# Computing integer angles and their quarter-turn shift on GpSimd instead of ScalarE and VectorE

## The chip, the cores and the metric

The kernel runs on one core of a Trainium2 chip. The metric is device time in microseconds (us). The engines are called PE (TensorE), ACT (ScalarE), DVE (VectorE), POOL (GpSimd) and SP (SyncE, which issues the DMAs).

## The reference, cut to what matters

A state-space convolution (S4) of 2048 steps and 512 channels with 128 states is mixed by a gate with a routed feed-forward update of two tokens. Only this part concerns the change:

```python
dt = jnp.exp(log_dt)[:, None]
A = A_re + 1j * A_im
logdA = dt * A                                          # (D=512, N=128)
l = arange(L) cast to bfloat16
P = jnp.exp(logdA[:, :, None] * l[None, None, :])       # complex powers
K = jnp.einsum("dn,dnl,dn->dl", C, P, dt * B).real      # the convolution's kernel
y = irfft(rfft(u padded) * rfft(K padded))              # long convolution
...
return g * a + (1 - g) * b
```

The kernel builds `P` as a product of two tables: lag t = t1 + t2, one table of exp(dt·A·t1), one of exp(dt·A·t2). Each entry is a magnitude (an exponential on ACT) times a sine or a cosine of an angle.

## The kernel before

The kernel describes its work as a list of operations with costs, and a list scheduler in the kernel's own source places them on the engines before anything is compiled; the engines then run fixed orders and wait on semaphores. A changed cost or engine therefore also changes the order. Channels come in two halves, `h` = 0 and 1.

The angles are 16-bit integers, 65536 to a turn, so that wrapping is free. There are 16 groups of four angles, eight groups for each half. `B16` holds the base angle as float32:

```python
def trig(h, angs, ts, neg):
    k = na[0] % 2                                   # two angle buffers, used in turn
    na[0] += 1
    a, ah, s = ARG[k], ARH[k], SNC[k]
    for i, t in enumerate(angs):                    # 4 scalings of 256, f32 -> int32
        SCL(a(0, 128, i * HC, (1, HC)), B16(0, 128, h * HC, (1, HC)), float(t), [B16], [(a, i)])
    ks = [(a, i) for i in range(4)]
    ...
    AC(so(0), lo, ACTF.Sin, ks, [(s, "s")], scale=SC16, tset=ts)      # sine of the low 16 bits
    w = a(0, 128, 0, (1, n))
    TS(w, w, 16384.0, ALU.add, ks, ks)              # a quarter turn: 1 add of 1024 int32
    AC(so(2), lo, ACTF.Sin, ks, [(s, "c")], scale=SC16, tset=ts)      # cosine
```

`SCL` may go to ACT or DVE, as the scheduler finds; `TS` is on DVE. The sines and cosines feed long rows of DVE multiplies (`TT`, two inputs in SBUF, bf16), of 2048, 1024, 512 or 1280 elements a partition:

```python
def TT(o, a, b, op, rd, wr, **k):
    return P.op(DVE, lambda h: h.tensor_tensor(out=o, in0=a, in1=b, op=op), rd, wr, cost=tt_cost(o, a, b), **k)
```

Memory is reused tightly. One reuse matters below: the second half's tables `TQ[1]` lie where the product table `KA[0]` of the first half lies.

```python
TQ = [... for i, o in enumerate((oE, oG))]
KA = [B("ka0", oG, 64 * 84 * 2), B("ka1", oE, 64 * 84 * 2)]
...
tab1(0, (1, 1)); forward(); tab2(0, (1, 1)); tab1(1, (1, 1)); xupd(); kgen(0); tab2(1, (1, 1)); ...; kgen(1); ...
```

So `tab2(1)` on DVE can't write before the results of `kgen(0)`, matmuls of the first half's tables whose products go to `KA[0]`, have been read out of there. PE runs the forward transform (`forward`), which needs no tables.

Of the kernel before, what the change touches and what calls it, by code (L numbers as in the profile page):

```python
# [14 lines left out]
ALU = mybir.AluOpType  # L15
AX = mybir.AxisListType

PE, ACT, DVE, POOL, SP = "pe", "act", "dve", "pool", "sp"
# [237 lines left out]
BLK, NBLK, HF, HC = 1024, 2, 2, 256  # L256
# [70 lines left out]
def bass_gated_mix__ssm_conv_s4__moe_arch_mod__prompt_kernel(nc, A_u, A_A_re, A_A_im, A_B_re, A_B_im, A_C_re, A_C_im, A_log_dt, A_Dskip,  # L327
# [24 lines left out]
    with ExitStack() as es:  # L352
# [6 lines left out]
        P = Prog()  # L359
# [18 lines left out]
        def nel(ap):  # L378
            r = 1
            for s, c in ap.ap[1:]:  # L380
                r *= c
            return r
# [5 lines left out]
        def TS(o, a, s1, op0, rd, wr, s2=None, op1=None, rate=0.5e-3, **k):  # L388
            c = 0.17 + nel(o) * rate
            if op1 is None:  # L390
                return P.op(DVE, lambda h: h.tensor_scalar(out=o, in0=a, scalar1=s1, scalar2=None, op0=op0), rd, wr, cost=c, **k)  # L391
            return P.op(DVE, lambda h: h.tensor_scalar(out=o, in0=a, scalar1=s1, scalar2=s2, op0=op0, op1=op1), rd, wr, cost=c, **k)
# [4 lines left out]
        def AC(o, a, func, rd, wr, scale=1.0, bias=0.0, **k):  # L397
            return P.op(ACT, lambda h: h.activation(out=o, in_=a, func=func, scale=scale, bias=bias), rd, wr,  # L398
                        cost=0.185 + nel(o) * 0.833e-3 + (0.09 if not isinstance(scale, float) else 0), **k)
# [4 lines left out]
        def SCL(o, a, c, rd, wr, **k):  # L404
            n = nel(o)
            return P.op((ACT, DVE), (lambda h: h.activation(out=o, in_=a, func=ACTF.Copy, scale=c), lambda h: h.tensor_scalar(out=o, in0=a, scalar1=c, scalar2=None, op0=ALU.mult)), rd, wr,  # L406
                        cost=(0.19 + n * 0.833e-3, 0.165 + n * (0.48e-3 if a.dtype == F32 else 0.245e-3)), **k)
        def DMA(pairs, rd, wr, nbytes, eng=SP, **k):
            return P.op(eng, lambda h: [h.dma_start(o, i) for o, i in pairs], rd, wr, cost=0.5 * len(pairs), n=len(pairs), nbytes=nbytes, dma=True, **k)

# [67 lines left out]
        def DQ(pairs, rd, wr, nbytes, **k):  # L478
            dp[0] -= 1e3
            return DMA(pairs, rd, wr, nbytes, prio=dp[0], **k)  # L480
# [60 lines left out]
        def trig(h, angs, ts, neg):  # L541
            k = na[0] % 2
            na[0] += 1
            a, ah, s = ARG[k], ARH[k], SNC[k]
            for i, t in enumerate(angs):
                SCL(a(0, 128, i * HC, (1, HC)), B16(0, 128, h * HC, (1, HC)), float(t), [B16], [(a, i)])
            ks = [(a, i) for i in range(4)]
            lo = bass.AP(ah.tensor, ah.offset, [[ah.ap[0][0], 128], [2 * HC, 4], [8, 64], [2, 4]])
            n = 4 * HC
            def so(k):  # L550
                return s(0, 128, k * n, (4, 4), (16, 64), (1, 4))
            AC(so(0), lo, ACTF.Sin, ks, [(s, "s")], scale=SC16, tset=ts)
            w = a(0, 128, 0, (1, n))
            TS(w, w, 16384.0, ALU.add, ks, ks)
            AC(so(2), lo, ACTF.Sin, ks, [(s, "c")], scale=SC16, tset=ts)
            if neg:
                SCL(s(0, 128, n, (1, n)), s(0, 128, 0, (1, n)), -1.0, [(s, "s")], [(s, "n")])
            return s
        def tab1(h, ts):
            for g in range(4):  # L560
                s = trig(h, ANG1[4 * g:4 * g + 4], ts[g // 2], True)
                n = 4 * HC
                ti, tr = TP[h]
                ek = [(tr, ("e", 4 * g + i)) for i in range(4)] + [(tr, ("e", 16 + 4 * g + i)) for i in range(4)]
                v = lambda b: b(0, 128, 16 * g, (64, 2), (128, 64), (1, 16))
                TT(v(ti), v(tr), s(0, 128, 0, (n, 2), (16, 64), (1, 16)), ALU.mult, ek + [(s, "s"), (s, "n")], [(ti, g)])
                TT(v(tr), v(tr), s(0, 128, 2 * n, (0, 2), (16, 64), (1, 16)), ALU.mult, [(s, "c")], ek)
# [17 lines left out]
        def tab2(h, ts):  # L585
# [3 lines left out]
            for g in range(4):  # L589
                s = trig(h, ANG2[4 * g:4 * g + 4], ts[g // 2], False)  # L590
                if g < 2:
                    im, re = [b_(0, 128, 16 * g, (4 * NJ, 64), (1, 16)) for b_ in (qi, qr)]
                    src = eb(0, 128, 16 * g, (32, 64), (1, 16))
                    ek = [(eb, ("e", 4 * g + i)) for i in range(4)]
                    ki, kr = (qi, ("s", g)), (qr, ("s", g))
                else:
                    im, re = [b_(0, 128, 16 * (g - 2), (32, 64), (1, 16)) for b_ in (bi, br)]
                    src = re
                    ek = [(br, ("e", 4 * (g - 2) + i)) for i in range(4)]
                    ki, kr = (bi, ("i", g)), (br, ("r", g))  # L600
                TT(im, src, s(0, 128, 0, (16, 64), (1, 16)), MUL, ek + [(s, "s")], [ki])
                TT(re, src, s(0, 128, 2 * n, (16, 64), (1, 16)), MUL, ek + [(s, "c")], [kr] + (ek if g > 1 else []))
                if g < 2:
                    v = lambda part: tq(part)(0, 128, 16 * g, (4 * NJ, 64), (4, 4), (1, 4))
                    w = lambda part: WW(0, 128, (1 - part) * D + h * HC, (4, 64), (0, 4), (1, 4))
                    cmul(h, v, v, w, n, [ki, kr], [WW], lambda p: [(ki, kr)[p]])
# [11 lines left out]
        def routing():  # L618
# [75 lines left out]
            for i, (W, k) in enumerate(((wg, [WG]), (wu, WU))):  # L694
# [7 lines left out]
                P.op(PE, ffn1, [*k, XS], [bb.buf], cost=56 * 0.026)  # L702
                CP(hb(i), bb(0, 128, 0, (1, 28)), [bb.buf], [(HB, i)])
            DMA([(WD(0, 128, 0, (D, 14), (1, D)), dr(B_w_down, 0, (D, 128), (128 * D, 14), (1, D)))], [], [WD], 1835008)
            AC(hb(2), hb(0), ACTF.Silu, [(HB, 0)], [(HB, 2)], tset=1)
            TT(hb(3), hb(2), hb(1), MUL, [(HB, 2), (HB, 1)], [(HB, 3)])
# [11 lines left out]
        def forward():  # L718
            np_ = [0]
            for blk in range(NBLK):  # L720
                for ft in range(4):
                    k = blk * 4 + ft
                    ng = NG[k % 2]
                    if k > 1:
                        DMA([(ng(0, 128, 0, (128, 8), (1, 128)), ngsrc(ft))], [], [ng], 262144, prio=2e5)
                    for pm in range(2):
                        pb = fwp[np_[0] % 2]
                        np_[0] += 1
                        for part in range(2):
                            def fw(h, blk=blk, ft=ft, pm=pm, pb=pb, ng=ng, part=part):  # L730
                                last = None
                                o = pb(0, 128, part * 512, (1, 512))
                                for par in range(2):
                                    for st in range(4):
                                        w = ng(0, 128, (st * 2 + part) * 128, (1, 128)) if par and pm else F(0, 128, ((par * 4 + st) * 2 + part) * 512 + ft * 128, (1, 128))
                                        last = h.matmul(o, w, U(0, 128, (blk * 8 + st * 2 + par) * D, (1, D)), start=(par + st == 0), stop=(par * 4 + st == 7 and blk == 0))  # L736
                                if blk:
                                    last = h.matmul(o, CB(0, 128, 640 if part == 0 else 512, (1, 128)),  # L738
                                                    X(0, 128, (1 - part) * 2048 + (pm * 4 + ft) * 256, (8192, 2), (1, 256)), start=False, stop=True)
                                return last  # L740
                            rd = [F, CB, ng] + [(U, blk * 8 + t) for t in range(8)]
                            if blk:
                                rd += [xk(hh, 0, 1 - part, pm, ft) for hh in range(2)]
                            P.op(PE, fw, rd, [(pb.buf, part)], cost=(8 + blk) * 0.217)
                        EV(X(0, 128, blk * 4096 + (pm * 4 + ft) * 256, (2048, 2), (8192, 2), (1, 256)), pb(0, 128, 0, (512, 2), (256, 2), (1, 256)),
                           [pb.buf], [xk(hh, blk, part, pm, ft) for hh in range(2) for part in range(2)])
# [204 lines left out]
```

## Time and profile before

206.42 us, median of three runs (206.23 to 206.93); the profiled span is 203.5 us.

| What | Value |
|---|---|
| DVE busy / PE busy / ACT busy / POOL busy | 171.3 / 163.9 / 141.1 / 3.4 us |
| angle scalings on ACT, on DVE | 44 x 407 ns, 20 x 284 ns |
| quarter-turn adds on DVE | 16 x 680 ns |
| DVE multiplies of 1024, of 2048 | 681 ns, 1216 ns |
| second half's `kgen` matmuls start | 137.56 us |

The window view, busy microseconds of each engine in chosen stretches of the kernel before (after the stretch: its length, then PE, PE weight loads, DVE, ACT, POOL with instruction counts, then the granted clock, the DMA share and GB/s):

```profile
40.00:60.00 20.00, 19.76 (x191) 10.13 (x192) 19.93 (x38) 18.90 (x31) 0.00 (x0) 1.00 0.42 119
60.00:80.00 20.00, 19.89 (x92) 9.10 (x93) 20.00 (x38) 19.62 (x32) 0.00 (x0) 1.00 0.13 30
80.00:104.60 24.60, 24.44 (x255) 14.43 (x257) 20.74 (x31) 22.48 (x38) 0.00 (x0) 1.00 0.25 89
104.60:116.70 12.10, 8.40 (x26) 2.56 (x25) 12.06 (x21) 12.03 (x21) 0.00 (x0) 0.72 0.53 228
116.70:137.60 20.90, 12.57 (x111) 10.31 (x110) 20.90 (x35) 8.27 (x9) 0.00 (x0) 0.91 0.00 1
```

From 40 to 104.6 us three engines are full. From 104.6 to 137.6 us DVE is full and PE is not.

The groups, kernel before (count, then busy us and mean ns of one, then idle time before and who ended it): first the page's group of all multiplies, then the groups by shape:

```profile
L387 DVE TENSOR_TENSOR AR<-AR 128x1024 bf16<-128x1024 bf16 (+7 forms) x184 | 135.7, 797 | 12.5 <-DMA AR<-in_A_A_re_dram 6.8
L387 DVE TENSOR_TENSOR AR<-AR 128x2048 bf16<-128x2048 bf16 x48 | 57.3, 1216 | 0.1
L387 DVE TENSOR_TENSOR AR<-AR 128x1024 bf16<-128x1024 bf16 x90 | 57.0, 681 | 5.2 <-ACT AR L398 4.4 <-PE ps L775 0.6
L406 ACT ACTIVATE AR<-AR 128x256 int32<-128x256 f32 x44 | 15.3, 407 | 0.1
L391 DVE TENSOR_SCALAR AR<-AR 128x1024 int32<-128x1024 int32 x16 | 10.9, 680 | 0.0
L406 DVE TENSOR_SCALAR AR<-AR 128x256 int32<-128x256 f32 x20 | 4.8, 284 | 1.9 <-ACT AR L398 1.8
```

The second and third are most of the table and product multiplies; the last three are what the change moves. The PE timeline, the line where the second half's `kgen`, matmuls of its tables, begins (start, length, and in brackets the idle time before it):

```profile
137.56 7.81 PE L756 MATMUL ps<-AR 128*128 128x84 bf16 x128 [7.60 <-DVE AR L387]
```

PE waited 7.60 us for a DVE multiply here. From this line to the end are 66 us.

### The profile page before, as it was taken

How to read it: one execution, taken by the hardware profiler on the slowest of the kernel's cores; microseconds unless marked ns; L12 is line 12 of the kernel's file. 1: busy time of each engine (PE TensorE's matmuls, PEld its weight loads, DVE VectorE, ACT ScalarE, POOL GpSimd, SP SyncE). 2: the span in 40 equal slices, each digit the busy share in tenths (PEclk: the TensorE clock that was granted, in tenths of full speed). 3: DMA queues.
4: the chain of work that ended last, by engine and by line, in shares of the span. 5: the costliest groups of instructions: out<-in, count | busy, mean ns of one | idle time of the engine just before them, and what ended most of it. 6: DMA issues, size and time to landing. Idle time of an engine off the chain costs nothing.

```text
span 203.5 us, 3609 instructions
## 1 busy us (share of the span) xinstructions
PE 163.9 (81%) x1479; PEld 108.6 (53%) x1490; DVE 171.3 (84%) x281; ACT 141.1 (69%) x232; POOL 3.4 (2%) x7
## 2 busy tenths in 40 slices
PE   0084799999999999999984999509889999809992
PEld 0073544774344444466550387408668888607881
DVE  0579545699999999999489999999999999999152
ACT  2599999989999999699999946406636654401400
POOL 6000000000000000000000000000000000000000
PEclk9997579999999999999997599966999999985998
DMA  5998999149202022000498000000280000303033
GB/s 86 271 323 364 307 410 358 33 121 293 53 0 55 0 52 52 0 3 0 135 435 362 0 5 0 0 0 3 61 354 0 3 0 0 106 0 103 0 103 103
DMA packets 22097, 23.17 MB, mean 114 GB/s; under 512 B 13121, under 2 KB 19394, under 8 KB 21442
## 3 DMA queue, kind: packets, MB, share of 16 engines
q1 hardware_dynamic: 20738, 22.63, 33.8%
q10 hardware_dynamic: 1344, 0.33, 1.4%
q8 instruction: 11, 0.18, 0.4%
q14 instruction: 4, 0.03, 0.0%
HBM read 19.02 MB, written 3.15 MB: 109 GB/s over the span
## 4 chain that ended last, share of the span: by engine, by line
PE 63%; DVE 22%; ACT 7%; DMA 4%; issue 1%; SPq 1%; DVEq 0%
PE ps L736 28%; DVE AR L387 20%; PE ps L841 12%; PE ps L791 6%; PE ps L756 5%; ACT AR L402 4%; DMA AR<-in_A_u_dram 4%; PE ps L769 3%; ACT AR L398 3%; PE ps L738 2%; PE ps L711 2%; PE ps L625 1%; PE ps L700 1%; SPq L483 1%; PE ps L637 1%
## 5 line engine op out<-in xcount | busy, mean ns | idle before, releaser
L387 DVE TENSOR_TENSOR AR<-AR 128x1024 bf16<-128x1024 bf16 (+7 forms) x184 | 135.7, 797 | 12.5 <-DMA AR<-in_A_A_re_dram 6.8
L398 ACT ACTIVATE AR<-AR 128x512 bf16<-128x512 f32 (+4 forms) x84 | 59.5, 769 | 5.4 <-DVE AR L391 2.1
L402 ACT ACTIVATE AR<-ps 128x1024 bf16<-128x1024 f32 (+4 forms) x56 | 44.0, 811 | 25.5 <-PE ps L791 12.8
L736 PE MATMUL ps<-AR 128*128 128x512 bf16 x248 | 59.0, 388 | 0.8 <-issue 0.5
L736 PEld LDWEIGHTS ps<-AR 128*128 128x128 bf16 x256 | 25.3, 100 | 30.2 <-issue 2.7
L841 PE MATMUL ps<-AR 128*128 128x256 bf16 x256 | 31.1, 287 | 5.9 <-DVE AR L387 5.9
L398 ACT ACTIVATE AR<-ps,AR 128x256 bf16<-128x256 f32 (+1 forms) x40 | 20.4, 565 | 18.8 <-PE ps L841 18.8
L841 PEld LDWEIGHTS ps<-AR 128*128 128x128 bf16 x256 | 26.3, 103 | 10.2 <-DVE AR L387 6.2
L791 PE MATMUL ps<-AR 128*128 128x256 bf16 x224 | 26.1, 274 | 1.7 <-ACT AR L402 1.7
L791 PEld LDWEIGHTS ps<-AR 128*128 128x128 bf16 x224 | 21.7, 99 | 6.1 <-ACT AR L402 3.1
L406 ACT ACTIVATE AR<-AR 128x256 int32<-128x256 f32 (+1 forms) x50 | 21.1, 484 | 0.1
L756 PE MATMUL ps<-AR 128*128 128x84 bf16 x256 | 13.5, 213 | 7.9 <-DVE AR L387 7.6
L756 PEld LDWEIGHTS ps<-AR 128*128 128x128 bf16 x256 | 12.0, 105 | 11.1 <-DVE AR L387 7.9
L625 PE MATMUL ps<-AR 128*128 128x128 bf16 x64 | 6.3, 278 | 12.5 <-DMA AR<-in_A_u_dram 10.8
L391 DVE TENSOR_SCALAR AR<-AR 128x1024 int32<-128x1024 int32 (+4 forms) x24 | 13.2, 552 | 0.3
L625 PEld LDWEIGHTS ps<-AR 128*128 128x128 bf16 x64 | 5.4, 127 | 13.1 <-DMA AR<-in_A_u_dram 10.8
L402 DVE CAST AR<-ps 128x1024 bf16<-128x1024 f32 (+1 forms) x7 | 8.0, 1142 | 3.2 <-remote 1.7
L867 PE MATMUL ps<-AR 128*128 128x512 bf16 x13 | 6.4, 492 | 3.6 <-ACT AR L398 3.6
L868 PE MATMUL ps<-AR 128*128 128x512 bf16 x16 | 7.6, 474 | 0.2
L406 DVE TENSOR_SCALAR AR<-AR 128x256 int32<-128x256 f32 (+1 forms) x22 | 5.6, 296 | 1.9 <-ACT AR L398 1.8
L769 PE MATMUL ps<-AR 128*32 128x128 bf16 (+1 forms) x96 | 6.4, 383 | 0.5 <-ACT AR L402 0.5
L402 DVE COPY AR<-ps 128x1024 bf16<-128x1024 bf16 (+1 forms) x7 | 4.7, 686 | 1.7 <-PE ps L625 1.4
(36 smaller groups left out, 57.0 us busy)
## 6 DMA issues: line engine op xcount, KB each, us to landing
AR<-c_ksp SPq DMA_DIRECT2D x1, 3584.0 KB, 13.5
AR<-in_A_u_dram SPq DMA_DIRECT2D x2, 1024.0 KB, 8.4
AR<-c_fwd SPq DMA_DIRECT2D x1, 2048.0 KB, 8.0
AR<-c_fwdn SPq DMA_DIRECT2D x8, 256.0 KB, 4.4
AR<-c_inv SPq DMA_DIRECT2D x1, 2048.0 KB, 8.9
out_dram<-AR SPq DMA_DIRECT2D x16, 128.0 KB, 2.2
AR<-in_B_w_gate_dram SPq DMA_DIRECT2D x1, 1792.0 KB, 11.2
AR<-in_B_w_up_dram SPq DMA_DIRECT2D x2, 896.0 KB, 11.5
```

The lines of the kernel that those rows point to most:

```text
L387: return P.op(DVE, lambda h: h.tensor_tensor(out=o, in0=a, in1=b, op=op), rd, wr, cost=tt_cost(o, a, b), **k)
L391: return P.op(DVE, lambda h: h.tensor_scalar(out=o, in0=a, scalar1=s1, scalar2=None, op0=op0), rd, wr, cost=c, **k)
L398: return P.op(ACT, lambda h: h.activation(out=o, in_=a, func=func, scale=scale, bias=bias), rd, wr, cost=0.185 + nel(o) * 0.833e-3 + (0.09 ...
L402: return P.op((ACT, DVE), (lambda h: h.activation(out=o, in_=a, func=ACTF.Copy), lambda h: h.tensor_copy(o, a)), rd, wr, cost=(0.185 + n * ...
L406: return P.op((ACT, DVE), (lambda h: h.activation(out=o, in_=a, func=ACTF.Copy, scale=c), lambda h: h.tensor_scalar(out=o, in0=a, scalar1= ...
L625: last = h.transpose(bb(0, 128, db * 256 + t_ * 128, (1, 128)), U(0, 128, (2 * q + t_) * D + db * 128, (1, 128)), IDN(0, (1, 128)))
L736: last = h.matmul(o, w, U(0, 128, (blk * 8 + st * 2 + par) * D, (1, D)), start=(par + st == 0), stop=(par * 4 + st == 7 and blk == 0))
L756: last = hh.matmul(pb(0, 128, (g - b0) * 84, (1, 84)), TP[h][1 - part](0, 128, g * 128, (1, 128)), TQ[h][1 - part](0, 128, g * 84, (1, 84) ...
L769: last = hh.matmul(pb(32 * g, 32, c4, (256, njg), (4, 64)), lw, KA[h](0, 128, c4 + 4 * (8 * bk + g), (16, njg), (84, 64)), start=True, sto ...
L791: last = hh.matmul(pb(0, 128, n * 256, (1, 256)), KP(0, 128, u * 2048 + tau * 128, (1, 128)), KC[h](0, 128, jg * 256, (1, 256)), start=(k ...
L841: last = hh.matmul(pb(0, 128, e * 256, (1, 256)), G(0, 128, ((par * 2 + part) * 4 + ft) * 512 + (2 * t2 + e) * 128, (1, 128)), X(0, 128, h ...
L868: return h.matmul(pb(0, 128, c0, (1, D)), OHR(0, 128, tb * 128, (1, 128)), ZB(0, 128, D, (1, D)), start=False, stop=True)
```

## The change

Intent: POOL is idle, so let it make the angles; ACT loses 15.3 us of work and DVE 15.7 us (4.8 + 10.9). The whole diff:

```diff
+        def PTS(o, a, s1, op0, s2, op1, rd, wr, **k):
+            return P.op(POOL, lambda h: h.tensor_scalar(out=o, in0=a, scalar1=s1, scalar2=s2, op0=op0, op1=op1), rd, wr, cost=0.2 + nel(o) * 1.0e-3, **k)
...
-                SCL(a(0, 128, i * HC, (1, HC)), B16(0, 128, h * HC, (1, HC)), float(t), [B16], [(a, i)])
+                PTS(a(0, 128, i * HC, (1, HC)), B16(0, 128, h * HC, (1, HC)), float(t), ALU.mult, 0.0, ALU.add, [B16], [(a, i)])
...
-            TS(w, w, 16384.0, ALU.add, ks, ks)
+            PTS(w, w, 16384.0, ALU.add, 1.0, ALU.mult, ks, ks)
```

The scheduler orders all engines anew with these costs.

## The prediction

> **What bounds the kernel now.** The window view shows PE, VectorE (DVE) and ScalarE (ACT) all close to full from 40 to 104.6 us (DVE 60.7 and ACT 61.0 of 64.6 us), then DVE 12.1 of 12.1 and 20.9 of 20.9 us up to 137.6 us, while PE idles there (21.0 busy of 33.0). The chain of waits agrees: PE to 104.6 us, DVE multiplies from there to 137.56 us, then PE starts the second kernel-table matmuls (L756), with one wait of 7.6 us on DVE. So building the sine/cosine tables on DVE, helped by ACT, sets when the second half starts; what is gained or lost before 137.6 us passes on to the end nearly in full, as far as DVE is what is relieved.
>
> **Removed.** Groups by form: 44 ACT scalings f32 to int32 of 256 (15.3 us, 407 ns each), 20 such on DVE (4.8 us, 284 ns), 16 DVE adds of 1024 int32 (10.9 us, 680 ns). DVE loses 15.7 us, ACT 15.3 us, nearly all between 40 and 116 us. The scheduler can also let ACT take some of the PSUM evictions that DVE does (1.2 us each on DVE).
>
> **Added.** The same 80 operations on GpSimd (POOL), which now runs only memsets (3.4 us). No POOL arithmetic is in the trace. Its memset of 2048 took 1.805 us, 0.88 ns an element. The Trainium skill, "GPSIMD Engine Reference", section 3.1, gives 769 ns for 512 elements of a tight one-input loop (1.5 ns an element). Estimate from these: 0.35 to 0.6 us for 256, 1.0 to 1.7 us for 1024: 2.4 to 4.1 us per group of four angles, 40 to 65 us in all. Sines start only after the exponentials (about 40 us), and two angle buffers allow only two groups ahead, so 14 of 16 groups run from 40 to 116 us.
>
> **The hidden cost.** The Trainium skill, "SBUF — State Buffer", section "Who interferes with whom", says a DVE instruction with two SBUF inputs contends with a GpSimd instruction that reads SBUF, and that the second to issue fully blocks. No line of this trace shows it yet. From 40 to 116.7 us DVE spends about 57 of 76.7 us in two-input multiplies with next to no gap. If the lock is total, each POOL operation waits out a multiply and then holds up the next: DVE gets back 30 to 50 us for the 15.7 removed, and each group's sine waits for five such turns. If it is partial, it roughly cancels. Without it, DVE reaches 137 us some 12 to 18 us earlier, limited then by ACT and by PE's forward matmuls.
>
> **Sum.** Total lock: 206 - 16 - a few for evictions + 30 to 50 = 215 to 240 us. No contention: about 190 us. Weighing these: 216 us, range 192 to 244. Faster by over 2%: 0.25; within 2%: 0.13; slower: 0.62.
>
> **What the profile would show.** POOL at 40 to 65 us busy, DVE's adds and both engines' scalings gone. If I am right: mean DVE multiply of 2048 or 1024 longer than 1216 and 681 ns (or gaps before them) where POOL is busy; DVE waiting for ACT sines and these for POOL; the second L756 matmuls start later than 137.6 us. After that the stages unchanged. If wrong: multiplies keep 1216 and 681 ns, and L756 restarts near 122 us.
>
> **What would make it wrong.** POOL's lock being brief or its operations very short; POOL operations far slower than estimated (then the sines wait for POOL and the time goes past 240 us); the scheduler, fed other costs, reordering the engines for good or ill by some us.

## The result, and the profile after

223.74 us, median of four runs (222.87 to 224.40), against 206.32 us for four runs of the kernel before. The ratio is 1.084 (95% interval 1.080 to 1.088). The change costs 8.4%.

The groups of the changed kernel that answer to the lines above:

```profile
L387 DVE TENSOR_TENSOR AR<-AR 128x1024 bf16<-128x1024 bf16 (+6 forms) x184 | 151.3, 886 | 19.4 <-ACT AR L398 7.1
L387 DVE TENSOR_TENSOR AR<-AR 128x1024 bf16<-128x1024 bf16 x90 | 65.3, 774 | 12.4 <-ACT AR L398 7.1 <-DMA AR<-park 4.3 <-PE ps L777 0.6
L387 DVE TENSOR_TENSOR AR<-AR 128x2048 bf16<-128x2048 bf16 x48 | 60.3, 1279 | 0.4
L409 POOL TENSOR_SCALAR AR<-AR 128x256 int32<-128x256 f32 x64 | 44.2, 700 | 15.7 <-ACT AR L398 7.2 <-DVE AR L387 5.7
L409 POOL TENSOR_SCALAR AR<-AR 128x1024 int32<-128x1024 int32 x16 | 21.5, 1348 | 45.3 <-ACT AR L398 44.6
```

The same multiplies take longer: 774 instead of 681 ns, 1279 instead of 1216 ns. All multiplies together (the first line, the page's group for L387, which joins the shapes) went from 135.7 to 151.3 us busy. DVE lost 15.7 us of angle work and got 15.6 us back in slower multiplies.

How a single multiply is stretched shows on the DVE and POOL timelines of the changed kernel. DVE first (start, length), a multiply that no POOL operation held up and two that were held up:

```profile
65.12 0.69 DVE L387 TENSOR_TENSOR AR<-AR 128x1024 bf16<-128x1024 bf16 x1 [0.59 <-ACT AR L398]
66.54 0.88 DVE L387 TENSOR_TENSOR AR<-AR 128x1024 bf16<-128x1024 bf16 x1
68.14 1.52 DVE L387 TENSOR_TENSOR AR<-AR 128x1024 bf16<-128x1024 bf16 x1
```

The POOL timeline: first operations that no DVE multiply held up, then the two that held up the two multiplies above:

```profile
9.58 0.89 POOL L409 TENSOR_SCALAR AR<-AR 128x256 int32<-128x256 f32 x2 [5.68 <-DVE AR L387]
53.91 1.04 POOL L409 TENSOR_SCALAR AR<-AR 128x1024 int32<-128x1024 int32 x1
66.16 0.72 POOL L409 TENSOR_SCALAR AR<-AR 128x256 int32<-128x256 f32 x1
67.76 1.36 POOL L409 TENSOR_SCALAR AR<-AR 128x1024 int32<-128x1024 int32 x1
```

The first line joins two scalings, 0.89 us together: the first 0.40 us, a gap of 0.08, the second 0.41. So POOL alone needs about 0.40 us for 256 elements and 1.04 us for 1024. The Trainium skill, "Perfetto Trace Analysis", section "GPSIMD Engine Instruction", warns that POOL spans are unreliable and advises the spacing of starts: the eight scalings near 10 us start 0.48 us apart, so that the span of 0.40 us leaves out at most 0.08 us of each. In company the scaling took 0.72 us and the add 1.36 us (0.32 us of waiting each, for the multiply that was running), and the *next* multiply was longer by 0.19 us (0.88 - 0.69) for a scaling and by 0.83 us (1.52 - 0.69) for an add.

The waits of the changed kernel (who waited for whom: us in total, times, longest), and the PE timeline's line for the second `kgen`:

```profile
ACT AR L398 <- POOL AR L409: 15.6, 12, 2.9
DVE AR L402 <- PE ps L758: 12.0, 1, 12.0
PE ps L738 <- ACT AR L402: 8.2, 6, 3.0
DVE AR L387 <- ACT AR L398: 7.1, 5, 2.8
```

```profile
156.33 7.81 PE L758 MATMUL ps<-AR 128*128 128x84 bf16 x128 [8.23 <-DVE AR L387]
```

ACT's sines wait for POOL; behind them wait the PSUM evictions in ACT's queue, and so PE (8.2 us); DVE waits for the sines (7.1 us, against 4.4 us before). The second `kgen` starts at 156.3 instead of 137.6 us, 18.8 us later, and from there to the end it is 66.3 us, against 66.0 before. Nearly all of the loss lies ahead of that line.

One more thing: DVE idles for 17 us near 104 to 122 us (12.0 and 4.3 us of it in the lines above), which it did not before. Is this the cause? It had to be tested.

### The profile page after: what moved, and what is told of

It is laid out like the page before. It is cut to its first block, busy times and chain, and to the rows that moved or that the text cites. A ratio compares the mean times of both kernels' runs of the same rounds, so it can differ in the third digit from the quotient of the medians. Undisturbed runs are those within 1.5% of the kernel's fastest.

```text
span 222.6 us, 3637 instructions
## 1 busy us (share of the span) xinstructions
PE 171.0 (77%) x1490; PEld 109.4 (49%) x1490; DVE 172.4 (77%) x243; ACT 131.0 (59%) x190; POOL 69.0 (31%) x87
## 4 chain that ended last, share of the span: by engine, by line
DVE 51%; PE 19%; POOL 11%; ACT 10%; DMA 3%; issue 2%; SPq 1%; DVEq 0%
DVE AR L387 50%; POOL AR L409 11%; ACT AR L398 9%; PE ps L843 7%; PE ps L738 4%; DMA AR<-in_A_u_dram 3%; PE ps L758 3%; PE ps L627 2%; PE ps L771 1%; ACT AR L402 1%; SPq L485 1%; ACT L242 1%; DVE AR L406 1%; PE ps L740 0%; PE ps L870 0%
## 5 line engine op out<-in xcount | busy, mean ns | idle before, releaser
L387 DVE TENSOR_TENSOR AR<-AR 128x1024 bf16<-128x1024 bf16 (+6 forms) x184 | 151.3, 886 | 19.4 <-ACT AR L398 7.1
L409 POOL TENSOR_SCALAR AR<-AR 128x256 int32<-128x256 f32 (+1 forms) x80 | 65.6, 829 | 61.0 <-ACT AR L398 51.8
L398 ACT ACTIVATE AR<-AR 128x512 bf16<-128x512 f32 (+4 forms) x84 | 59.3, 772 | 27.2 <-POOL AR L409 15.6
L738 PE MATMUL ps<-AR 128*128 128x512 bf16 x256 | 67.0, 417 | 8.2 <-ACT AR L402 8.2
L402 ACT ACTIVATE AR<-ps 128x1024 bf16<-128x1024 f32 (+4 forms) x60 | 47.8, 823 | 32.5 <-PE ps L793 12.8
L738 PEld LDWEIGHTS ps<-AR 128*128 128x128 bf16 x256 | 26.1, 106 | 43.9 <-ACT AR L402 11.6
L843 PEld LDWEIGHTS ps<-AR 128*128 128x128 bf16 x256 | 26.1, 102 | 10.7 <-DVE AR L387 6.7
L793 PEld LDWEIGHTS ps<-AR 128*128 128x128 bf16 x224 | 21.5, 98 | 5.7 <-ACT AR L402 3.1
L758 PE MATMUL ps<-AR 128*128 128x84 bf16 x256 | 14.2, 220 | 11.9 <-DVE AR L387 11.6
L758 PEld LDWEIGHTS ps<-AR 128*128 128x128 bf16 x256 | 12.6, 110 | 15.4 <-DVE AR L387 12.4
L402 DVE CAST AR<-ps 128x1024 bf16<-128x1024 f32 (+1 forms) x3 | 2.9, 983 | 12.6 <-PE ps L758 12.0
L627 PEld LDWEIGHTS ps<-AR 128*128 128x128 bf16 x64 | 5.5, 129 | 12.4 <-DMA AR<-in_A_u_dram 11.0
L869 PE MATMUL ps<-AR 128*128 128x512 bf16 x16 | 6.2, 385 | 4.6 <-ACT AR L398 4.6
L740 PE MATMUL ps<-AR 128*128 128x512 bf16 x16 | 6.6, 411 | 0.0
L870 PE MATMUL ps<-AR 128*128 128x512 bf16 x16 | 6.1, 379 | 0.0
L869 PEld LDWEIGHTS ps<-AR 128*128 128x128 bf16 x16 | 1.6, 97 | 8.8 <-ACT AR L398 8.4
```

Source lines behind the costliest of these rows:

```text
L398: return P.op(ACT, lambda h: h.activation(out=o, in_=a, func=func, scale=scale, bias=bias), rd, wr, cost=0.185 + nel(o) * 0.833e-3 + (0.09 ...
L402: return P.op((ACT, DVE), (lambda h: h.activation(out=o, in_=a, func=ACTF.Copy), lambda h: h.tensor_copy(o, a)), rd, wr, cost=(0.185 + n * ...
L409: return P.op(POOL, lambda h: h.tensor_scalar(out=o, in0=a, scalar1=s1, scalar2=s2, op0=op0, op1=op1), rd, wr, cost=0.2 + nel(o) * 1.0e-3, ...
L627: last = h.transpose(bb(0, 128, db * 256 + t_ * 128, (1, 128)), U(0, 128, (2 * q + t_) * D + db * 128, (1, 128)), IDN(0, (1, 128)))
L738: last = h.matmul(o, w, U(0, 128, (blk * 8 + st * 2 + par) * D, (1, D)), start=(par + st == 0), stop=(par * 4 + st == 7 and blk == 0))
L740: last = h.matmul(o, CB(0, 128, 640 if part == 0 else 512, (1, 128)), X(0, 128, (1 - part) * 2048 + (pm * 4 + ft) * 256, (8192, 2), (1, 25 ...
```

## The experiments

Two theories and two rivals:

- **Contention**: a POOL operation that reads SBUF and a DVE multiply with two SBUF inputs keep each other out. The contention is what the Trainium skill, "SBUF — State Buffer", section "Who interferes with whom", states ("A DVE instruction with two SBUF inputs contends with a GpSimd instruction that reads SBUF, not with one that only writes it").
- **Slow answers**: POOL simply takes longer (0.40 and 1.04 us alone, against 0.28 or 0.41 and 0.68 us), and sines wait.
- **Order**: the new static order is bad; the idle stretch of DVE is planned.
- On the side of the gain: **DVE sets the pace** (the prediction), or **PE caps it**.

Ten kernels were run. In four of them the angles are wrong on purpose; the comparison with the reference does not see these angles, and says nothing for them. The runs of the kernel before beside them had medians of 206.09 us (first job), 206.84 us (second) and 206.40 us (third). Since the last 66 us never change, the table gives the start of the first and of the second `kgen` on PE, read from the traces.

| Run | Median us | Ratio to before (95%) | first / second `kgen` at us | profiled span |
|---|---|---|---|---|
| before | 206.4 | 1 | 87.6 / 137.6 | 203.5 |
| the change | 223.74 | 1.084 (1.080 to 1.088) | 102.5 / 156.3 | 222.6 |
| e1, POOL only writes | 204.74 | 0.993 (0.989 to 0.997) | 88.0 / 137.4 | 203.2 |
| e9, POOL only writes, slowly | 207.85 | 1.004 (1.000 to 1.008) | 89.4 / 139.7 | 205.8 |
| e3, old order | 220.01 | 1.068 (1.066 to 1.070) | 98.2 / 152.5 | 218.9 |
| e4, scalings only | 221.66 | 1.071 (1.068 to 1.075) | 101.9 / 154.0 | 220.0 |
| e5, adds only | 221.90 | 1.075 (1.068 to 1.082) | 97.7 / 153.2 | 218.8 |
| e2a, angles nearly free, old order | 204.89 | 0.995 (0.990 to 0.999) | 88.2 / 137.1 | 202.5 |
| e2b, the same, new order | 203.59 | 0.988 (0.985 to 0.991) | 85.6 / 135.2 | 201.1 |
| e6, bystander (flawed) | 219.04 | 1.059 (1.055 to 1.062) | 88.9 / 151.5 | 217.0 |
| e10, bystander mended | 211.26 | 1.023 (1.019 to 1.027) | 89.7 / 143.6 | 209.2 |
| e7, eight early scalings only | 206.25 | 0.999 (0.996 to 1.002) | 88.1 / 138.1 | 204.1 |

### e1: same order, same waits, but POOL reads nothing

```diff
 def PTS(o, a, s1, op0, s2, op1, rd, wr, **k):
-    return P.op(POOL, lambda h: h.tensor_scalar(out=o, in0=a, ...), rd, wr, cost=0.2 + nel(o) * 1.0e-3, **k)
+    return P.op(POOL, lambda h: h.memset(o, 7), rd, wr, cost=0.2 + nel(o) * 1.0e-3, **k)
```

> The changed kernel with every GpSimd angle operation replaced by a memset of the same tile: it still waits and is waited for, and every engine keeps its order, but it reads nothing from SBUF (the result is wrong on purpose). Lock theory (a GpSimd operation that reads SBUF and a VectorE multiply with two SBUF inputs exclude each other): the multiplies fall back to about 681 ns (1024) and 1216 ns (2048), the total of L387 from 151 to about 136 us, and the time to 202 to 208 us. Order theory (the new static order, which leaves VectorE idle for 17 us near 104 to 122 us, costs the time): stays above 216 us. Latency theory (GpSimd is only slow to answer the sines): in between, as memsets are a little shorter, 210 to 218 us, with multiplies unchanged from those of the changed kernel.

Measured: 204.74 us. The groups by shape of this run:

```profile
L387 DVE TENSOR_TENSOR AR<-AR 128x2048 bf16<-128x2048 bf16 x48 | 57.4, 1220 | 1.8 <-ACT AR L398 1.5
L387 DVE TENSOR_TENSOR AR<-AR 128x1024 bf16<-128x1024 bf16 x90 | 57.0, 689 | 8.9 <-DMA AR<-park 4.3 <-ACT AR L398 3.7 <-PE ps L777 0.6
L409 POOL MEMSET AR<- 128x256 int32 x64 | 17.4, 316 | 22.4 <-ACT AR L398 16.7 <-DVE AR L387 5.6
L409 POOL MEMSET AR<- 128x1024 int32 x16 | 15.4, 960 | 54.2 <-ACT AR L398 53.7
```

The multiplies are back at 689 and 1220 ns, and the whole loss is gone, in exactly the changed kernel's order on PE, DVE, ACT and the DMA queues. The idle stretch of DVE is still there, 4.3 us of it for a DMA (above) and 9.6 us for PE:

```profile
DVE AR L402 <- PE ps L758: 9.6, 1, 9.6
```

Yet the run is no slower than the kernel before. The order theory falls as the main cause. The memsets are also somewhat shorter than the real operations, so slow answers are not ruled out yet.

### e9: POOL as slow as in the changed kernel, but reading nothing

Each POOL operation became two memsets, one waiting for the other: 256 + 256 elements for a scaling, 384 + 1024 for an add. The extra memset is inserted after scheduling, so that the order stays.

```diff
+            p = P.op(POOL, lambda h: h.memset(o, 7), rd, wr, cost=0.2 + nel(o) * 1.0e-3, **k)
+            first = o if nel(o) == HC else bass.AP(o.tensor, o.offset, [o.ap[0], [1, 384]])
+            twice[p.idx] = lambda h: h.memset(first, 5)    # placed ahead of p, after scheduling
```

> As the changed kernel and in its order, but each GpSimd operation is a pair of memsets that read nothing and together take about as long as the operation took in the changed kernel (0.70 and 1.35 us; wrong on purpose). It keeps GpSimd's slow answers and takes away what it does to the multiplies. If the slow answers alone cost the time: 216 to 224 us. If the stretched multiplies alone do: 203 to 207 us. I expect a part: 206 to 214 us, with L387 back at about 136 us and ScalarE still waiting for GpSimd 8 us or more.

Measured: 207.85 us, ratio 1.004. This run's page, the line of all multiplies (L410, in what follows, is POOL's line here):

```profile
L387 DVE TENSOR_TENSOR AR<-AR 128x1024 bf16<-128x1024 bf16 (+6 forms) x184 | 135.6, 801 | 20.5 <-ACT AR L398 7.6
```

And its waits (engine, line, what it waited for: us in total, times, longest):

```profile
ACT AR L398 <- POOL AR L410: 10.8, 13, 1.6
DVE AR L387 <- ACT AR L398: 7.6, 6, 2.8
```

A pair took about as long as the contended operation: 0.69 us for a scaling (0.316 + 0.318 and a gap of 0.06 us between the two), 1.44 us for an add (0.420 + 0.966 + 0.06), against 0.70 and 1.35 us. By the spacing of starts the imitation is somewhat too quick: the pairs near 10 us start 0.62 us apart, two scalings held up in the changed kernel 0.80 us (66.16 and 66.96 us). ACT still waits 10.8 us for POOL (15.6 in the changed kernel) and DVE 7.6 us for ACT, yet only 2 to 3 us are lost against e1 (3.1 us by the medians, from two jobs on two chips; 1.1 points, or 2.2 us, by the ratios). So answers as slow as these cost 2 to 3 us; the other 16 us or so (223.74 - 207.85; 8 points by the ratios) come with POOL's *reads*: with the stretched multiplies, and with what the reads delay POOL's answers beyond these pairs. No run splits these two.

### e3: the old order, with POOL doing the angles

The kernel before is scheduled as it was; then the 80 operations are handed to POOL in the order of their planned starts. PE, DVE, ACT and the DMA queues keep their order (with the angle operations gone).

```diff
         P.span = P.schedule()
+        for o in P.ops:
+            if o.idx in to_pool:
+                P.order[o.eng].remove(o)
+                o.eng, o.fn, o.alt = POOL, to_pool[o.idx], None
+                P.order[POOL].append(o)
+        P.order[POOL].sort(key=lambda o: o.start)
+        ... positions counted anew ...
```

> GpSimd does all 80 angle operations, but TensorE, VectorE, ScalarE and the DMA queues keep the order of the kernel before (scheduled as before, the angle operations then moved over). Lock theory: about as slow as the changed kernel, 216 to 228 us, since the multiplies are stretched the same way. Order theory: most of the loss is gone, 200 to 212 us.

Measured: 220.01 us, 1.068. Most of the loss stays (6.8 of 8.4%). The rest, 1.6 points, is what the new order may account for; the two ratios come from different jobs.

### e4 and e5: one half of the change each

```diff
 e4:  scalings PTS(...) on POOL; the add stays  TS(w, w, 16384.0, ALU.add, ks, ks)
 e5:  scalings stay SCL(...); the add  PTS(w, w, 16384.0, ALU.add, 1.0, ALU.mult, ks, ks)
```

> Only the 64 scalings go to GpSimd; the 16 adds stay on VectorE. Lock theory: a scaling of 256 costs the multiply that it meets about 0.19 us (as the changed kernel's trace shows: 0.69 to 0.88 us), so at most 12 us more on VectorE against 4.8 us taken off it; and each group's sines still wait for four GpSimd turns: 210 to 220 us. If the adds were the whole cost: 202 to 207 us.

> Only the 16 adds go to GpSimd; the scalings stay on ScalarE and VectorE. Lock theory: an add of 1024 costs the multiply that it meets about 0.83 us, so at most 13 us more against 10.9 us taken off VectorE, and each second sine waits about 0.7 us longer: 205 to 213 us. If the scalings were the whole cost: 202 to 207 us.

Measured: 221.66 and 221.90 us. Both lie above my ranges: either half alone costs nearly as much as both. The multiplies were stretched far less than in the full change (the page's L387 group is 140.1 us in e4 and 139.6 us in e5, against 151.3). Both have a new order of their own, and no run took only POOL's reads out of them, so what follows is read from their traces and not shown by a test. Where did the time go? The groups of POOL in e5, and one operation of e5 on the POOL timeline with what DVE did meanwhile:

```profile
L409 POOL TENSOR_SCALAR AR<-AR 128x1024 int32<-128x1024 int32 x16 | 36.0, 2258 | 88.0 <-ACT AR L398 88.0
```

```profile
90.29 8.22 POOL L409 TENSOR_SCALAR AR<-AR 128x1024 int32<-128x1024 int32 x1 [6.73 <-ACT AR L398]
```

```profile
90.45 7.16 DVE L387 TENSOR_TENSOR AR<-AR 128x2048 bf16<-128x2048 bf16 x8
100.71 1.23 DVE L387 TENSOR_TENSOR AR<-AR 128x2048 bf16<-128x2048 bf16 x1 [3.10 <-ACT AR L398]
```

An add that takes 1.04 us alone took 8.22 us. It started while DVE was in an unbroken row of multiplies, got next to nothing done until the row ended at 97.61 us (90.45 + 7.16), and finished 0.90 us after that. The add behind it ended at 99.52 us. Only then did ACT, which had waited 5.48 us, begin the next cosine, and so DVE stood idle for 3.10 us. Two more adds took 5.10 and 5.19 us; in e4 one scaling took 4.72 us. This is contention with the other loser: DVE keeps POOL out, and pays for it when its own next input depends on POOL. In e5 ACT waits 12.0 us for POOL and DVE's multiplies 11.8 us for ACT. In e4 (L391 is its adds, on DVE):

```profile
ACT AR L398 <- POOL AR L409: 25.3, 12, 5.4
DVE AR L391 <- ACT AR L398: 10.6, 6, 2.9
DVE AR L387 <- ACT AR L398: 6.1, 4, 2.8
```

In the kernel before, DVE waits 6.2 us for ACT (4.4 and 1.8 us). Not only multiplies were held up: 3 of the 16 integer adds that e4 leaves on DVE, with one input each, took 0.88 to 0.89 us, where one takes 0.68 us in the kernel before.

### e6 and e10: POOL work that nobody needs

The kernel before in its own order, plus 52 POOL scalings of 256 beside the first half's table multiplies, whose results nobody uses. In e6 each is released by one multiply, and all write an unused 1 KB.

```diff
 def TT(o, a, b, op, rd, wr, **k):
-    return P.op(DVE, ...)
+    p = P.op(DVE, ...)
+    if by[0]:      # while the first half's tables are built
+        q = P.op(POOL, lambda h: h.tensor_scalar(out=DUM(...), in0=B16(0, 128, 0, (1, HC)), ...), [B16], [DUM], cost=0.5)
+        q.deps.add(p.idx)
+    return p
```

> The kernel before, same order, plus 52 GpSimd scalings of 256 that nobody waits for (into an unused 1 KB), each released by one multiply of the first half's tables. Only the contention is added. Lock theory: about 0.19 us on each multiply met, so the total of L387 goes from 136 to 143 to 147 us, the first kernel-table matmuls start 5 to 10 us later than at 87.6 us, and the time is 209 to 217 us. If multiplies and GpSimd reads do not disturb each other: 206 us as before.

Measured: 219.04 us, above my range, but the run is flawed. My 1 KB lay in the place of `TQ[1]`, which is written later, and so DVE waited 12.6 us for POOL to be through with it. It doesn't measure contention alone. It did bring the first sight of a POOL operation of 34.84 us.

e10 mends it: 256 bytes that overlay nothing, and all 52 operations released at once.

```diff
+        DUM = small("dum", 256, mybir.dt.uint8)        # at the end of the small buffers
-        q.deps.add(p.idx)
+        by.append(p.idx); q.deps.add(by[1])            # all after the first multiply
```

> The bystander run mended: its 52 GpSimd operations of 256 now write 256 bytes that overlay no other tile, so that truly nobody waits for them, and all are released at once by the first multiply of the tables, one after the other, as a pressing GpSimd queue would be. If GpSimd gets its turn between multiplies (as in the changed kernel): about 0.19 us on each multiply met, L387 up by 5 to 10 us, and the time 210 to 217 us, though nothing depends on GpSimd. If VectorE's unbroken runs shut it out (one operation of the first bystander run took 34.84 us): L387 as before and 206 to 208 us.

Measured: 211.26 us, 1.023 (1.019 to 1.027): slower, clear of the noise, though the interval lies on both sides of a bar of 2%. POOL's group in e10, and its longest operation on the timeline:

```profile
L390 POOL TENSOR_SCALAR AR<-AR 128x256 uint8<-128x256 f32 x52 | 72.3, 1390 | 43.8 <-DVE AR L388 39.5
```

```profile
60.62 34.84 POOL L390 TENSOR_SCALAR AR<-AR 128x256 uint8<-128x256 f32 x1
```

The DVE timeline of e10 at the end of that operation:

```profile
94.52 0.67 DVE L397 TENSOR_SCALAR AR<-AR 128x1024 int32<-128x1024 int32 x1
95.12 1.21 DVE L408 CAST AR<-ps 128x1024 bf16<-128x1024 f32 x1
```

Both faces are in one run. Where POOL got its turn between multiplies, it stretched them: all multiplies together (their durations summed from the trace) took 151.1 us instead of 146.7, 4.4 us more. DVE's own integer adds and scalings grew too, from 10.9 to 11.9 and from 5.7 to 6.5 us (five adds took 0.88 to 0.89 us). The second `kgen` came 6.0 us later, and the time rose by 4.9 us (211.26 - 206.40), although nothing depends on POOL. So DVE work that is stretched on this path is paid for nearly in full. From 60.6 to 95.1 us POOL was shut out: DVE ran multiplies, integer adds and scalings back to back, and the operation that needs 0.40 us ended 0.34 us after DVE began a copy *out of PSUM* (`AR<-ps`), the first instruction in that row with no SBUF input. DVE lost nothing while POOL stood outside (its multiplies of 1024 took 0.67 us).

### e2a and e2b: what could be gained at most

The kernel before with its 80 angle operations cut from 256 or 1024 columns to 4, left on ACT and DVE. A POOL memset at the start fills the buffers. e2a keeps the order of the kernel before (it pins the old costs for the scheduler, not shown here); in e2b the scheduler knows of the short costs.

```diff
-                SCL(a(0, 128, i * HC, (1, HC)), B16(0, 128, h * HC, (1, HC)), float(t), [B16], [(a, i)])
+                SCL(a(0, 128, i * HC, (1, 4)), B16(0, 128, h * HC, (1, 4)), float(t), [B16], [(a, i)])
-            w = a(0, 128, 0, (1, n))
+            w = a(0, 128, 0, (1, 4))
```

> The kernel before with its 80 angle operations cut to 4 columns on the engines and in the order where they are (wrong on purpose; the buffers are filled once by a GpSimd memset at the start). It shows what taking the angle work off ScalarE and VectorE could bring at most in this order. If VectorE alone set the pace up to 137.6 us, as the prediction had it, 15.7 us of VectorE and 15.3 us of ScalarE work vanish and the time is 188 to 195 us. If TensorE, full from 24 to 104 us, caps it: 200 to 206 us.

> As the run before, but the kernel's own scheduler knows that the angle operations are short and orders the engines anew. VectorE as sole bound: 186 to 195 us. TensorE and the memory shared between the first kernel table and the second half's tables as cap: 199 to 206 us, with a VectorE idle stretch of over 8 us before the second half's tables.

Measured: 204.89 and 203.59 us. The short operations are not free: in e2a they still take 5.9 us of DVE instead of 15.7 and 8.6 us of ACT instead of 15.3. But with 10 us less on DVE and 7 us less on ACT, only 0.5 to 1.2% is won, and e1, with none of the angle work on either, wins 0.7%. Two waits of e2b say where it stopped (L758 is `kgen`):

```profile
DVE AR L402 <- PE ps L758: 8.2, 2, 7.6
DVE AR L387 <- DMA AR<-park: 4.3, 1, 4.3
```

DVE is done early and then idles for PE. The forward matmuls end at 101.2 us in e2a and 99.7 us in e2b, 100.7 us before, interleaved with the first `kgen`, which starts at 88.2 us in e2a and 85.6 us in e2b (87.6 before); `tab2(1)` may not write before its results are read, because it overlays `KA[0]`. Whether another place for `TQ[1]` would free more of the gain was not tried. The idle stretch of DVE in the changed kernel is this same wait, on top of the delay: the window view has PE busy for 17.5 of 17.5 us there (104.4 to 121.9 us), since much of the forward transform was still to do. It follows from the late tables; it is not what made them late.

### e7: a try for a version better than both

The order of the kernel before, and only the eight scalings of the first two groups on POOL, which run near 10 us where DVE is not yet in its rows of multiplies (the device of e3, for the first two groups only: `if na[0] <= 2`).

> A try for something better than both: order of the kernel before, and only the eight scalings of the first two groups, which run near 10 us where VectorE is not yet in its run of multiplies, go to GpSimd. They took 0.40 us each there in the changed kernel. Frees 1.5 us of VectorE ahead of the copies of the transposed input, near 10 us. If those copies set the start: 204.5 to 206 us; if not, 206 us as before. The runs with nearly free angle work (203.6 and 204.9 us) say that no more is to be had.

Measured in five rounds: 206.25 us, ratio 0.9986 (0.9955 to 1.0017). POOL took 404 ns each and disturbed nothing (multiplies at 682 and 1216 ns), but nothing is gained either. None of the runs with less angle work gained more than 1.2%.

## Why the prediction was right or wrong

The time (223.74 us) lies in the stated range (192 to 244) and the direction is right; the point, 216 us, was 7.7 us low. Two terms of the sum were mis-sized, and they partly offset each other, so that the nearness of the point is partly luck: with the DVE times as measured, the sum would have been 206 - 15.7 + 15.6, about 206 us, and no loss at all. That is the prediction's own branch for a partial lock ("it roughly cancels"), and it did not cancel. The contention was real; what made it a loss is that the work taken off DVE was worth almost nothing, while the stretch was paid for.

1. **"What is gained or lost before 137.6 us passes on to the end nearly in full, as far as DVE is what is relieved."** Right for losses: in every run the second `kgen` is followed by 65.4 to 66.5 us, and e10 lost 4.9 us for the 4.4 us by which its multiplies, and 1.8 us by which its adds and scalings, were stretched. For gains it promised far too much.
2. **"No contention: about 190 us", with DVE "some 12 to 18 us earlier".** Wrong. e1 has no contention and took 204.7 us; e2a and e2b have much less angle work and took 204.9 and 203.6 us. The window table showed the reason before the change: PE was busy for 64.1 of the 64.6 us from 40 to 104.6 us. I named PE's matmuls as a limit, but did not size it. The term "- 16" for the removed work should have been about minus 2.
3. **POOL's own durations**, estimated at 0.35 to 0.6 and 1.0 to 1.7 us and 40 to 65 us in all. Right: 0.40 and 1.04 us alone, 65.6 us in all with the waiting. The figure of the Trainium skill used for it ("GPSIMD Engine Reference", section 3.1: 769 ns for 512 elements) gives, as an estimate, 0.38 us for 256, near the 0.40 us measured, but 1.54 us for 1024, where 1.04 us was measured; the memset's 0.88 ns an element was the better guide there.
4. **"If the lock is total ... DVE gets back 30 to 50 us."** Mis-sized. A scaling held the next multiply for 0.19 us, not for its 0.40 us, and an add for 0.83 of its 1.04 us. At most that makes 64 x 0.19 + 16 x 0.83 = 25 us (an estimate from these numbers); the group L387 grew by 15.6 us, since not every operation held up a multiply.
5. **What would show it right**: "mean DVE multiply of 2048 or 1024 longer" (1279 and 774 ns, yes); "DVE waiting for ACT sines and these for POOL" (7.1 and 15.6 us, yes); "the second L756 matmuls start later" (156.3 us, yes); later stages unchanged (66.3 against 66.0 us, yes).
6. **The scheduler's reordering** was named as a risk "of some us": e3 puts it at about 1.6 points.
7. **Not foreseen**: that POOL can be shut out for many multiplies in a row. I had it wait out one multiply for each operation. In e4 and e5 the waits that follow from it are larger than the stretch (DVE's wait for ACT is 16.7 us in e4, its multiplies grew by 4.4 us); their new orders were not tested apart.

The balance as the runs give it: taking the angle work off (e1) wins about 1.5 us; POOL's slower answers (e9 against e1) cost 2 to 3 us; its SBUF reads (the change against e9, in the same order) cost about 16 us; with the old order the whole change costs 3 to 4 us less (e3). The parts do not add up over the two halves of the change (e4, e5); a POOL operation that does not stretch DVE can be delayed by it instead, which is the likely reason. What decides whether POOL gets its turn between two multiplies or is shut out until the row ends stays open: in the changed kernel no operation took over 2.01 us, in e4, e5, e6 and e10 some took 4.7 to 34.8 us, at similar moments within a multiply: a scaling of the changed kernel that came 0.05 us after a multiply had begun got its turn at the next one (at 65.18 us), one of e4 that came 0.04 us after waited 4.72 us in all (at 83.02 us).

## What to carry to other kernels

An idle engine is not a free engine: before moving elementwise work to GpSimd, look at what VectorE runs at that time, and if it is long rows of two-input multiplies, expect either them or GpSimd to be held up (here one-input integer adds on VectorE were held up as well). First bound the gain by making the work nearly free where it is (two cheap runs here showed 1%), because with three full engines, relieving two of them may win next to nothing, as here. To tell contention from latency and from order, keep order and waits and take away only the reads: a memset in the place of the operation did that here.

## What the Trainium skill lacked or had wrong

- "SBUF — State Buffer", section "Who interferes with whom": its rule that a two-input VectorE instruction contends with a GpSimd instruction that reads and not with one that only writes is confirmed (multiplies of 1024 at 774 ns beside reads, 689 ns beside memsets in the same order). The word of its section "🔬 SBUF: two separate sides", that the one that starts first gets the ports "for the whole instruction", is too strong here if an instruction is taken to last as long as its span in the profile: a GpSimd operation of 0.40 us held a multiply up by 0.19 us, one of 1.04 us by 0.83 us, each 0.21 us less than its own length.
- The same page, section "🎯 Summary: rules for kernel authors", says that the second to issue blocks "until the first finishes". It lacks that GpSimd can stay blocked through a whole unbroken row of VectorE instructions: 34.84 us for an operation of 0.40 us, until VectorE read from PSUM; 8.22 us for one of 1.04 us, until VectorE ran out of work.
- "GPSIMD Engine Reference": no duration for `tensor_scalar`. These runs show 0.40 us for 256 elements float32 to int32, and 1.04 us for 1024 int32 in place, with 0.08 us between one scaling and the next; memsets of int32 took 0.316 us for 256 and 0.96 us for 1024 by their spans (in e1, memsets of 256 in a row start 0.25 us apart).
- The same page, section 4.1, advises VectorE for elementwise work and calls one-input operations on GpSimd "roughly line-rate": 1.04 us against VectorE's 0.68 us for the same add (on GpSimd with a multiply by 1.0 behind it). The advice holds in this case, but mostly for a reason that this section does not give: the contention with VectorE (about 16 us), not the slower operation (2 to 3 us).
